# Attention values in two float16 parts with a power-of-two scale per head pair, reciprocals taken for two steps at once, and a new table of constants

## The chip, the cores and the metric

The kernel runs on one core of a Trainium2 chip. The core has five engines that run beside each other, each through its own list of instructions in order: TensorE (PE in the profile; its weight loads, PEld, overlap its matmuls), VectorE (DVE), ScalarE (ACT), GpSimd (POOL) and SyncE (SP), which issues nearly all DMAs here. The metric is the device time of one execution in microseconds (us), the lower the better. With one core there is one span, from the first to the last instruction that the profiler saw.

## The reference, cut to what matters

```python
# q, k, v: (4, 8, 576, 64) float32; tau 0.02; weights drawn as float64: w_in (512, 2048), w_out (2048, 512), two sets
def _attn_ref(q, k, v, tau):
    scores = q @ k.T / np.sqrt(64)
    thresh = scores.max(-1) - tau
    scores = np.where(scores >= thresh, scores, -1e9)
    attn = np.exp(scores - scores.max(-1))
    attn = attn / (attn.sum(-1) + 1e-09)
    return attn @ v
x = attn_out.transpose(0, 2, 1, 3).reshape(2304, 512)
x = np.maximum(x @ w_in, 0) ** 2 @ w_out                 # first layer
h = x @ w_in2;  return np.maximum(0.01 * h, h) @ w_out2  # second layer
```

A score is kept if it lies within tau of its row's largest; the softmax is over what is kept.

## The kernel before, in words

**Attention.** The 32 heads are taken as 16 head pairs (4 batches of 4 pairs), and a pair as 9 steps of 128 query rows (four per head, and one in which the last 64 rows of both heads lie together), 144 steps in all. `step` is one of them: TensorE makes 128x576 scores (`s`), VectorE takes the row maximum negated (`nb`, L539), ScalarE the exponential (`e`, L540), VectorE or GpSimd the threshold (`th`, L541 or L542), VectorE in one instruction masks and sums (`e` and `sum`, L544), then `t` = (sum + 1e-9)/32768 (`UP` is 32768; L547), and VectorE its reciprocal `r` (L549). The scaled row is split in two float16 parts `P` (high, then low as e\*r minus high, L587, or by two instructions at L297 to L310), and SyncE issues a DMA that transposes both parts into `PT`.

**Values.** Pairs 0 to 5 are in `nat`: scores in full float32 from `KH` alone. Pairs 6 to 15 have their q and k split in two parts each (`Q`, `KH` and `KL`). Pairs 0 to 4 (`nav` is 5) multiply the probabilities with `v` in float32, transposed on TensorE (L565, L566, L631). The other 11 pairs have `v` in three bfloat16 parts: the upper halves of `VA` and of `VA`'s remainder lie side by side as 128 columns, and the third part is `VB`, 64 columns. `prep` makes them with two subtractions over 128x640 that GpSimd or VectorE does. `values` is called for each head and each of its two column ranges (256 and 320 query rows), 44 times for these 11 pairs. Its list of products:

```python
        prods = [(slice(0, P), slice(0, w), j, hi, j) for j in range(NH)]
        prods += [(slice(0, P), slice(0, w), NH + j, hi, j) for j in range(MAIN)]
        prods += [((lo3, up3)[j % 2], slice(0, w), j, low, j) for j in range(MAIN)]
        prods += [(r, c_, MAIN, low, MAIN) for r, c_ in ((lo3, slice(0, half)), (up3, slice(half, w)))]
```

The first two lines are nine matmuls of 128 weight columns; the last two are six of 64, which go by turns to the two halves of the PSUM bank `o` (a ring of one). ScalarE then copies one half out (`tmp`, L639), VectorE adds the other (`xs`, L644), and SyncE writes `x1d` in DRAM.

**Layers.** All products of the layers are three passes of two-part operands. d_ff is 16 blocks. While attention runs, `ffn` does blocks 0 to 11 (`NFA`) of the first layer for the first 1792 tokens, in 7 pieces of 256 tokens (L675 is h, L701 is y), as fillers of TensorE. Behind the attention, the second phase (L811 h, L857 y) does all 16 blocks for the last 512 tokens, the missing blocks 12 to 15 for the others, and the second layer. Weights come as float64 and are put together from their two 32-bit words (`w_block`: L349, L350, L352, L354, then a rounded copy and the rest).

**Order.** No order is written by hand. `Plan.order` takes every operation with its assumed cost on each engine that may do it, and a priority, and lays them out one after the other; an engine with several choices is weighed by `price`. The program's order on each engine is the result, and it is fixed at build time. So a change in `CFG` or in a cost moves instructions everywhere.

Of the kernel before, what the change touches and what calls it, by code (L numbers as in the profile page):

```python
# [63 lines left out]
class Plan:  # L64
# [32 lines left out]
    def order(self):  # L97
# [58 lines left out]
        while len(done) < len(self.ops):  # L156
# [47 lines left out]
            else:  # L204
# [5 lines left out]
                free[e] = o.end - OVER.get(e, 0.0)  # L210
# [29 lines left out]
def mm(n):  # L240
    return (n + 5.5) / 2400.0
# [15 lines left out]
def tile_kernel(ctx: ExitStack, tc: tile.TileContext, qT, kT, vv, w1, w2, tau, eye, out):  # L257
# [25 lines left out]
    const.tile([P, 40], F32, name="rim")  # L283
# [40 lines left out]
    ca = const.tile([P, 1], F32, name="ca")  # L324

# [613 lines left out]
```

## Time and profile before

| what | value |
|---|---|
| runs before, us | 1086.04, 1094.08, 1093.3 (median 1093.3) |
| the profiled execution's own time, us | 1087.9 |
| its span, us | 1086.1 |
| granted TensorE clock over the span | 1.000 |
| PE busy, us (share) | 1059.4 (98%) |
| DVE busy, us | 732.8 (67%) |
| ACT busy, us | 509.1 (47%) |
| POOL busy, us | 342.1 (31%) |

The times are of whole executions; the span of the profiled one is 1.8 us less than its own time. The shares are means over parts of the program that have different limits: attention with fillers, and then layers alone. Matmuls are pipelined, so the durations of neighbours overlap; how far apart two of them start tells what one takes.

### The profile page before, as it was taken

What the parts mean: (1) busy time and instruction counts of PE and PEld (TensorE: products, weight loads), DVE (VectorE), ACT (ScalarE), POOL (GpSimd) and SP (SyncE); (2) the same over time, 40 slices, a digit from 0 to 9 for tenths busy, and PEclk for the clock granted to TensorE, in tenths of its full rate; (3) what the DMA queues carried; (4) which work ended last, traced back from release to release, by engine and by line L of the source; (5) the groups of instructions that cost most, each with busy time, mean ns of one, the idle gap of its engine ahead of it and who ended that gap; (6) DMA issues with size and microseconds to landing.
All of it is one profiled execution on the core that took longest, in us unless ns stands there. A gap on an engine that the chain in (4) does not pass through costs nothing.

```text
span 1086.1 us, 17711 instructions
## 1 busy us (share of the span) xinstructions
PE 1059.4 (98%) x6343; PEld 886.1 (82%) x6343; DVE 732.8 (67%) x1557; ACT 509.1 (47%) x902; POOL 342.1 (31%) x421
## 2 busy tenths in 40 slices
PE   8988999999999999999999999999999999999998
PEld 4555778888998889989888888888888888888887
DVE  7999898788988898756999975763423433433343
ACT  6899878876776788735343431221211111111121
POOL 5765778889886676410000000000000000000000
PEclk9999999999999999999999999999999999999999
DMA  7444449998888896745644543610100100010010
GB/s 196 122 133 144 137 108 193 181 171 171 169 171 149 172 169 119 142 83 180 227 138 155 181 147 123 225 41 0 70 8 1 39 20 1 1 40 1 1 40 20
DMA packets 186983, 119.16 MB, mean 110 GB/s; under 512 B 146064, under 2 KB 164624, under 8 KB 186896
## 3 DMA queue, kind: packets, MB, share of 16 engines
q1 hardware_dynamic: 186528, 117.82, 44.3%
q8 instruction: 50, 0.82, 0.3%
q10 hardware_dynamic: 368, 0.21, 0.1%
q14 instruction: 37, 0.30, 0.1%
HBM read 70.98 MB, written 17.83 MB: 82 GB/s over the span
## 4 chain that ended last, share of the span: by engine, by line
PE 65%; DVE 1%; ACT 1%; issue 0%; POOL 0%; ACTq 0%; POOLq 0%; DVEq 0%
PE h L811 26%; PE y L857 26%; PE h L675 5%; PE y L701 5%; PE o L627 2%; PE s L529 2%; DVE e L544 0%; DVE nb L539 0%; DVE P L308 0%; ACT e L540 0%; ACT P L554 0%; DVE gl L308 0%; DVE P L587 0%; ACT tmp L639 0%; POOL t L547 0%
## 5 line engine op out<-in xcount | busy, mean ns | idle before, releaser
L823 DVE TENSOR_TENSOR r<-h,r 128x512 f32<-128x512 f32 (+1 forms) x80 | 51.0, 638 | 211.4 <-ACT r L822 211.4
L822 ACT ACTIVATE r<-h 128x512 f32<-128x512 f32 (+1 forms) x80 | 44.5, 557 | 313.1 <-PE h L811 310.6
L310 POOL TENSOR_TENSOR xl<-xr,xh 128x512 fp32r<-128x512 f32 (+1 forms) x11 | 12.7, 1157 | 418.3 <-ACT xh L297 253.5
L544 DVE SCALAR_TENSOR_TENSOR e<-s,th,e 128x576 f32<-128x576 f32 x144 | 116.8, 814 | 31.5 <-ACT e L540 27.4
L529 PE MATMUL s<-KH,Q 128*128 128x288 f32 (+1 forms) x440 | 121.1, 368 | 10.1 <-DVE e L544 6.6
L540 ACT ACTIVATE e<-s,nb 128x576 f32<-128x576 f32 x144 | 106.7, 742 | 38.5 <-DVE nb L539 22.5
L539 DVE TENSOR_REDUCE nb<-s 128x1 f32<-128x576 f32 x144 | 107.8, 750 | 12.4 <-PE s L529 11.3
L529 PEld LDWEIGHTS s<-KH,Q 128*128 128x128 f32 (+1 forms) x440 | 73.6, 183 | 30.6 <-issue 12.3
L308 DVE TENSOR_TENSOR gl<-r,gh 128x512 fp32r<-128x512 f32 (+1 forms) x129 | 85.6, 664 | 8.2
L587 DVE SCALAR_TENSOR_TENSOR P<-e,r,P 128x576 f16<-128x576 f32 x59 | 57.1, 970 | 2.8 <-ACT P L554 1.7
L819 ACT ACTIVATE r<-h 128x512 f32<-128x512 f32 (+1 forms) x32 | 18.2, 573 | 86.4 <-PE h L811 80.1
L627 PE MATMUL o<-PT,VA 128*128 128x320 f16 (+1 forms) x396 | 56.5, 287 | 0.4 <-DVE xs L644 0.4
L529 PE MATMUL s<-KL,Q 128*128 128x288 f32 x200 | 55.8, 294 | 0.0
L299 DVE CAST gh<-r 128x512 fp32r<-128x512 f32 (+1 forms) x103 | 43.8, 425 | 15.9 <-ACT r L684 7.8
L310 POOL TENSOR_TENSOR gl<-r,gh 128x512 fp32r<-128x512 f32 (+1 forms) x25 | 32.7, 1309 | 58.7 <-issue 45.2
L352 DVE SCALAR_TENSOR_TENSOR wraw<-wraw 128x512 int32<-128x512 int32 x64 | 48.9, 765 | 1.7 <-ACT wraw L349 0.6
L349 ACT ACTIVATE wraw<-wraw 128x512 f32<-128x512 f32 x64 | 43.0, 681 | 9.9 <-DMA wraw<-w 9.7
L354 DVE SCALAR_TENSOR_TENSOR wraw<-wraw 128x512 int32<-128x512 int32 x64 | 45.9, 717 | 0.6
L542 POOL TENSOR_SCALAR th<-nb,ca 128x1 f32<-128x1 f32 x75 | 33.3, 444 | 37.0 <-DVE nb L539 29.3
L627 PEld LDWEIGHTS <-VA 128*128 128x128 bf16 x396 | 35.2, 98 | 10.8 <-issue 0.4
L554 ACT ACTIVATE e<-e,r 128x576 f32<-128x576 f32 x51 | 39.4, 776 | 7.5 <-DVE r L549 6.9
L310 POOL TENSOR_TENSOR P<-e,P 128x576 f16<-128x576 f32 x29 | 38.7, 1339 | 8.5 <-ACT P L297 7.6
(616 smaller groups left out, 3044.5 us busy)
## 6 DMA issues: line engine op xcount, KB each, us to landing
wraw<-w SPq DMA_DIRECT2D x64, 512.0 KB, 4.1
wraw<-qT SPq DMA_DIRECT2D x20, 288.0 KB, 4.2
wraw<-kT SPq DMA_DIRECT2D x20, 288.0 KB, 4.4
out<-yo SPq DMA_DIRECT2D x18, 256.0 KB, 2.0
VA<-vv SPq DMA_DIRECT2D x32, 128.0 KB, 2.8
x2d<-yo SPq DMA_DIRECT2D x16, 256.0 KB, 3.3
xr<-x2d SPq DMA_DIRECT2D x4, 1024.0 KB, 5.8
y1d<-ys SPq DMA_DIRECT2D x14, 256.0 KB, 2.8
```

What stands on the lines that cost most here:

```text
L308: alts.append(("V", dve(n), lambda: nc.vector.tensor_tensor(out=o(), in0=a(), in1=b(), op=alu), kind + "*"))
L310: alts.append(("G", pool2(n), lambda: nc.gpsimd.tensor_tensor(out=o(), in0=a(), in1=b(), op=alu), kind))
L529: nc.tensor.matmul(ps.get()[r, g, 0:S2], lhsT=o.Q.get()[:, q], rhs=(kk.get() if o.KL else f32(kk.get()))[:, g_(g)], start=k == 0 or not o. ...
L539: op(("V", 0.75, lambda: nc.vector.tensor_reduce(out=nb.get(), in_=pv(), axis=AX.XY, op=ALU.max, negate=True)), [ps], [nb], i + CFG["pd1"] ...
L540: op(("A", 0.74, lambda: nc.scalar.activation(e.get(), pv(), AF.Exp, bias=nb.get(), scale=1.0)), [ps, nb], [e], i + CFG["pex"], True)
L544: op(("V", 0.82, lambda: nc.vector.scalar_tensor_tensor(out=e.get(), in0=pv(), scalar=th.get(), in1=e.get(), op0=ALU.is_ge, op1=ALU.mult, ...
L587: op(("V", 0.8, lambda: nc.vector.scalar_tensor_tensor(out=lo(), in0=ev(), scalar=r_.get(), in1=hi(), op0=ALU.mult, op1=ALU.subtract), "*" ...
L627: nc.tensor.matmul(ps.get()[r, c_], lhsT=f_(v), rhs=parts16(pt)[:, j, c_], start=(k == 0), stop=k >= len(prods) - 2)
L675: nc.tensor.matmul(ps.get()[:, i], lhsT=a.get()[:, kc * P:(kc + 1) * P], rhs=x.get()[:, kc], start=(i == 0 and q == 0 and kc == 0), stop=( ...
L701: nc.tensor.matmul(yp[m // 2].get()[:, m % 2], lhsT=a.get()[:, c], rhs=x.get()[:, i], start=(f + i == 0 and q == 0 and m % 2 == 0), stop=( ...
L811: nc.tensor.matmul(ps.get()[:, 0:n], lhsT=a.get()[:, kc * P:(kc + 1) * P], rhs=x.get()[:, kc, 0:n], start=(q == 0 and kc == 0), stop=(q == ...
L857: nc.tensor.matmul(o(), lhsT=l, rhs=r, start=(first and q == 0), stop=(last and q == 2))
```

## The change

- **Values.** `prep` now only loads `VA`; a new `split`, called four steps into the pair before, makes two float16 parts of v. VectorE takes the largest absolute value of each partition (`vmax`), TensorE adds these over the partitions (a matmul with a 128x128 tile of ones into the bank `o`), VectorE makes a power of two of it (`vbound`) and its reciprocal (`vscale`), and the inverse scale (`vback`) is applied where `values` copies out. The products are nine matmuls a call; the six of `VB` are gone.
- **Reciprocals.** `sum`, `t` and `r` are 128x2 and serve two steps. `step` makes the even step's sum, the odd step's `t` and `r` are for both, and what follows (`rest`) is recorded behind the odd step. `th` is one subtraction.
- **Scale of the scores.** It is no longer multiplied into k by an instruction of its own for the split pairs (`wraw` by `qsc`, L416 or L417), but into q where q is rounded, and the rest of q is one VectorE instruction (it was GpSimd's or VectorE's).
- **Choice of engine.** The first conversion step of weights may go to GpSimd, their rounding too.
- **Constants.** All of `CFG`; `eb` (buffers of `e`) is 4, and was 3; `nf` gives 8 blocks for the last 256-token piece in the first phase, the other 4 go to the second phase; `xsg0` and `xsg` let ScalarE and GpSimd do more of the copies out (`xs`).

```diff
-    pd1=0.001, pex=-0.455, pd2=0.23, ph=4.551, pl=-0.358, hu=False, bg=2.696, lead=3.299, w0=24.867, wstep=2.436, fend=1.021, tol=0.448,
-    hor=-0.24, xlead=5.45, nb=3, eb=3, pb=3, ptb=3, kvb=3, nat=[0, 1, 2, 3, 4, 5], nav=5, two=False, vb=2, tmb=1, gb=2, xb=1, w2step=0.586,
+    lead1=1.422, xsg0=[1, 2], lbm=8, lb=[[1, 3, 7], [0], [1, 4], [0, 1, 6]], xsm=4, xsg=[1, 2], dq=1.924, xu=False, pqk=-4.818, pd1=-0.132,
+    pex=0.418, pd2=-0.108, ph=4.738, pl=-0.721, hu=False, bg=5.042, lead=4.267, w0=19.675, wstep=2.136, fend=1.005, tol=0.271, hor=-0.444,
+    xlead=5.567, nb=3, eb=4, pb=3, ptb=3, kvb=3, nat=[0, 1, 2, 3, 4, 5], nav=5, two=False, vb=2, tmb=1, gb=2, xb=1, w2step=-1.195,
+    nf=[12, 12, 12, 8], wo=1.672, slack=0, slackd=0.939, wrb=3, r1b=1, xrb=1,
...
-            op(times(kr.get, 2 * S), [kr], [kr], at(2))
             for h in range(2):
-                op(rnd(lambda h=h: qs(h), lambda h=h: q3()[:, h], S), [qr], [Q], at(2))
+                op(times(lambda h=h: qs(h), S, lambda h=h: q3()[:, h]), [qr], [Q], at(2))
             for h in range(2):
-                op(sub(lambda h=h: qs(h)[D:P], lambda h=h: q3()[D:P, h], lambda h=h: f32(qs(h)[D:P]), S), [qr, Q], [Q], at(3 + h))
+                op(("V", dve(S), lambda h=h: nc.vector.scalar_tensor_tensor(
+                    out=qs(h)[D:P], in0=q3()[D:P, h], scalar=qsc[D:P], in1=f32(qs(h)[D:P]), op0=ALU.mult, op1=ALU.subtract), "*"), [qr, Q], [Q], at(3 + h))
...
-        op(sub(lambda: va.get()[:, :, :, 1], lambda: va.get()[:, :, :, 0], lambda: up()[:, :, :, 0], nv), [va], [va], at(11))
-        op(sub(lambda: vb.get(), lambda: va.get()[:, :, :, 1], lambda: up()[:, :, :, 1], nv), [va], [vb], at(13))
+        op(("V", dve(nv), lambda: nc.vector.tensor_reduce(out=mx.get(), in_=va.get(), axis=AX.XYZ, op=ALU.max, apply_absolute_value=True)), [va], [mx], at(10))
+        st = val("ps_o", "o", 1, [P, 512], F32)
+        op(("T", 0.25, lambda: nc.tensor.matmul(st.get()[:, 0:1], lhsT=ones, rhs=mx.get(), start=True, stop=True)), [mx, ones_v], [st], at(10))
+        op(("V", 0.15, lambda: nc.vector.tensor_scalar(out=bd.get(), in0=st.get()[:, 0:1], scalar1=1e-25, scalar2=2.0 ** -14, op0=ALU.max, op1=ALU.mult)), [st], [bd], at(10))
+        op(("V", 0.15, lambda: nc.vector.tensor_scalar(out=bd.get().bitcast(I32), in0=bd.get().bitcast(I32), scalar1=0x7F800000, scalar2=None, op0=ALU.bitwise_and)), [bd], [bd], at(10))
+        op(("V", 0.158, lambda: nc.vector.reciprocal(out=sc.get(), in_=bd.get())), [bd], [sc], at(10))
...
+           [va, sc], [v16], at(11))
+        op(("V", dve(nv), lambda: nc.vector.scalar_tensor_tensor(out=v2(), in0=va.get(), scalar=sc.get(), in1=v1(), op0=ALU.mult, op1=ALU.subtract), "*"),
+           [va, sc, v16], [v16], at(13))
...
-        op([(g, c_, lambda eng=eng: eng.tensor_scalar(out=t_.get(), in0=sm.get(), scalar1=1e-9, scalar2=1.0 / UP, op0=ALU.add, op1=ALU.mult), "t")
-            for g, c_, eng in (("V", 0.146, nc.vector), ("G", 0.19, nc.gpsimd))], [sm], [t_], i + CFG["pd2"], True)
-        op(("V", 0.158, lambda: nc.vector.reciprocal(out=r_.get(), in_=t_.get())), [t_], [r_], i + CFG["pd2"], True)
+        if k:
+            op([(g, c_, lambda eng=eng: eng.tensor_scalar(out=t_.get(), in0=sm.get(), scalar1=1e-9, scalar2=1.0 / UP, op0=ALU.add, op1=ALU.mult), "t")
+                for g, c_, eng in (("V", 0.148, nc.vector), ("G", 0.192, nc.gpsimd))], [sm], [t_], i + CFG["pd2"], True)
+            op(("V", 0.16, lambda: nc.vector.reciprocal(out=r_.get(), in_=t_.get())), [t_], [r_], i + CFG["pd2"], True)
+        return lambda: rest(i, n, h, t, o, ps, e, r_, k)
...
         def av(k0, k1):
             for k in range(k0, k1):
-                r, c_, j, f_, v = prods[k]
-                nc.tensor.matmul(ps.get()[r, c_], lhsT=f_(v), rhs=parts16(pt)[:, j, c_], start=(k == 0), stop=k >= len(prods) - 2)
+                nc.tensor.matmul(ps.get()[:, 0:w], lhsT=o.V16.get()[:, k if k < NH else k - NH, h].rearrange("p a d -> p (a d)"),
+                                 rhs=parts16(pt)[:, k, 0:w], start=(k == 0), stop=(k == NB - 1))
```

What it moves is seen in the order of the built programs. On TensorE, a call of `values` with 320 columns among layer matmuls, before (`s` scores, `o` the output bank, `w0ih` a weight block's part; the nine pairs of rows on `VA` stand once, and of the six on `VB` the first and the last):

```order
L675 MATMUL h<-xh,w0ih 128x256 x4
L627 LDWEIGHTS VA
L627 MATMUL o<-PT,VA 128x320
...
L627 LDWEIGHTS VB
L627 MATMUL o<-PT,VB 64x320
...
L627 MATMUL o<-PT,VB 64x160
L529 MATMUL s<-KH,Q_1831 128x288
```

and now, where the one-column matmul for a later pair's scale stands a little ahead of such a call:

```order
L733 MATMUL y_2561<-gh,w9ol 128x256
L507 MATMUL o<-vmax,ones 128x1
L556 MATMUL s<-KH,Q_2498 128x288
L556 MATMUL s<-KL,Q_2498 128x288
...
L654 LDWEIGHTS V_2774
L654 MATMUL o<-PT,V_2774 128x320
...
L733 MATMUL y_2553<-gh,w10oh 128x256
```

The rows on `VB` have gone, and a row on `vmax` and `ones` has come, in the same bank.

On VectorE, some steps in the middle of attention, before (numbers are buffers):

```order
L539 TENSOR_REDUCE nb_3606<-s_3592 128x1
L308 TENSOR_TENSOR P16_2_110<-e_3546,P16_2_110 128x576
L549 RECIPROCAL r_3632<-t_3617 128x1
L539 TENSOR_REDUCE nb_3636<-s_3614 128x1
L544 SCALAR_TENSOR_TENSOR e_3622,sum_3655<-s_3592,th_3624,e_3622 128x576
L547 TENSOR_SCALAR t_3670<-sum_3655 128x1
L549 RECIPROCAL r_3676<-t_3670 128x1
L544 SCALAR_TENSOR_TENSOR e_3658,sum_3678<-s_3614,th_3666,e_3658 128x576
```

and now:

```order
L505 TENSOR_REDUCE vmax_3505<-VA_3355 128x1
L620 SCALAR_TENSOR_TENSOR P16_1_110<-e_3357,r_3409,P16_1_110 128x576
L579 RECIPROCAL r_3528<-t_3514 128x2
L573 SCALAR_TENSOR_TENSOR e_3495,sum_3533<-s_3449,th_3497,e_3495 128x576
L566 TENSOR_REDUCE nb_3544<-s_3507 128x1
L508 TENSOR_SCALAR vbound_3554<-o_3542 128x1
L568 TENSOR_TENSOR th_3562<-ca_81,nb_3544 128x1
L509 TENSOR_SCALAR vbound_3554<-vbound_3554 128x1
L566 TENSOR_REDUCE nb_3565<-s_3548 128x1
L510 RECIPROCAL vscale_3575<-vbound_3554 128x1
L573 SCALAR_TENSOR_TENSOR e_3560,sum_3533<-s_3507,th_3562,e_3560 128x576
L577 TENSOR_SCALAR t_3593<-sum_3533 128x2
```

One reciprocal of two columns stands for two steps (both `e` rows add to `sum_3533`), and the chain for the scale of `v` is threaded through the steps of the pair before.

## Rows read from the trace of the kernel before

**Rows 1.** Busy time by stage: us, PE, PEld, DVE, ACT, POOL, PEclk, DMA share, GB/s

```profile
0.00:142.00 142.00, 126.81 (x725) 80.86 (x726) 123.28 (x288) 120.22 (x200) 92.98 (x137) 1.00 0.50 144
142.00:471.00 329.00, 322.03 (x2589) 288.15 (x2589) 280.37 (x665) 247.25 (x452) 243.46 (x276) 1.00 0.83 159
471.00:526.00 55.00, 54.25 (x447) 51.81 (x446) 35.84 (x69) 23.20 (x41) 2.44 (x4) 1.00 0.52 158
526.00:1086.00 560.00, 556.33 (x2587) 465.32 (x2585) 293.28 (x539) 118.41 (x211) 3.19 (x4) 1.00 0.20 67
```

**Rows 2.** Who waited for whom, 142 to 471 us: total, times, longest

```profile
DVE e L544 <- ACT e L540: 24.2, 41, 2.0
```

**Rows 3.** Timeline of TensorE around one 320-column call: start, us, instruction

```profile
267.13 1.40 PE L627 MATMUL o<-PT,VA 128*128 128x320 f16 x9
268.46 0.53 PE L627 MATMUL o<-PT,VB 128*64 128x320 f16 x6
268.92 0.39 PE L701 MATMUL y<-gh,w1oh 128*128 128x256 f32 x1
269.14 0.28 PE L701 MATMUL y<-gl,w1oh 128*128 128x256 f32 x1
269.26 0.28 PE L701 MATMUL y<-gh,w1ol 128*128 128x256 f32 x1
```

**Rows 4.** The same, behind a 256-column call

```profile
291.12 0.47 PE L627 MATMUL o<-PT,VB 128*64 128x256 f16 x6
291.51 0.39 PE L675 MATMUL h<-xh,w9ih 128*128 128x256 f32 x1
```

**Rows 5.** Groups by line and shape, whole span: busy us, mean ns, idle before

```profile
L627 PE MATMUL o<-PT,VB 128*64 128x320 f16 x88 | 10.2, 311 | 0.0
L627 PE MATMUL o<-PT,VB 128*64 128x256 f16 x88 | 9.0, 285 | 0.0
```

**Rows 6.** Timeline of TensorE in the first stage: float32 transposes

```profile
62.53 0.60 PE L565 MATMUL pt<-eye_sb,e 128*128 128x128 f32 x4
62.97 0.27 PE L566 MATMUL pt<-eye_sb,e 128*128 128x128 f32 x1
```

**Rows 7.** Groups of VectorE by line and shape, 142 to 471 us

```profile
L587 DVE SCALAR_TENSOR_TENSOR P<-e,r,P 128x576 f16<-128x576 f32 x58 | 56.3, 973 | 2.8 <-ACT P L554 1.7 <-POOL P L553 0.9
L549 DVE RECIPROCAL r<-t 128x1 f32<-128x1 f32 x99 | 15.7, 159 | 2.9 <-POOL t L547 1.1
L541 DVE TENSOR_SCALAR th<-nb,ca 128x1 f32<-128x1 f32 x59 | 12.4, 211 | 0.6
L644 DVE SCALAR_TENSOR_TENSOR xs<-o,tmp 64x320 f32<-64x320 f32 x21 | 10.0, 478 | 3.8 <-ACT tmp L639 3.1
L547 DVE TENSOR_SCALAR t<-sum 128x1 f32<-128x1 f32 x64 | 9.4, 148 | 1.0
L644 DVE SCALAR_TENSOR_TENSOR xs<-o,tmp 64x256 f32<-64x256 f32 x21 | 8.7, 412 | 3.0 <-ACT tmp L639 2.8
L308 DVE TENSOR_TENSOR Q<-wraw,Q 64x576 fp32r<-64x576 f32 x3 | 3.5, 1150 | 0.1
```

**Rows 8.** Busy time by stage, one stretch of the second stage

```profile
250.00:300.00 50.00, 49.37 (x405) 45.15 (x404) 47.22 (x115) 34.85 (x63) 43.69 (x49) 1.00 0.88 170
```

**Rows 9.** Timeline of VectorE: the low part of P twice

```profile
260.74 0.80 DVE L587 SCALAR_TENSOR_TENSOR P<-e,r,P 128x576 f16<-128x576 f32 x1
262.56 1.47 DVE L587 SCALAR_TENSOR_TENSOR P<-e,r,P 128x576 f16<-128x576 f32 x1
```

**Rows 10.** Timeline of GpSimd at the second of these

```profile
262.13 1.28 POOL L310 TENSOR_TENSOR gl<-r,gh 128x512 fp32r<-128x512 f32 x1
```

**Rows 11.** Groups of GpSimd by line and shape, 142 to 471 us

```profile
L310 POOL TENSOR_TENSOR Q<-wraw,Q 64x576 fp32r<-64x576 f32 x17 | 27.0, 1594 | 2.0 <-DVE Q L299 0.8
```

**Rows 12.** Timeline of VectorE: the last part of the second phase's first input

```profile
513.04 0.68 DVE L308 TENSOR_TENSOR xl<-xr,xh 128x512 fp32r<-128x512 f32 x1
```

**Rows 13.** Timeline of TensorE: the second phase's first matmuls

```profile
518.79 1.09 PE L811 MATMUL h<-xh,w0ih 128*128 128x512 f32 x4
```

More of the change, by code (lines that the diff above doesn't have):

```diff
@@ L209, in order @@
                     o.end = port["V"] = max(o.end, port["G"] - 0.13 + cost[o])
-                free[e] = o.end - OVER.get(e, 0.0)
+                free[e] = o.end - (OVER.get(e, 0.0) if o.alts[0][3:] != ("x",) else 0.0)
             for g, *_ in o.alts:
@@ L324, in tile_kernel @@
     ca = const.tile([P, 1], F32, name="ca")
+    ones = const.tile([P, P], F32, name="ones")
+    ones_v = Val()
     eye_v = Val()
@@ L492, in prep @@
             return
-        op(sub(lambda: va.get()[:, :, :, 1], lambda: va.get()[:, :, :, 0], lambda: up()[:, :, :, 0], nv), [va], [va], at(11))
-        op(sub(lambda: vb.get(), lambda: va.get()[:, :, :, 1], lambda: up()[:, :, :, 1], nv), [va], [vb], at(13))
+        v16 = o.V16 = val("att", "V16", CFG["vb"], [P, NH, 2, 2, D], F16)
+        mx, bd, sc, us = (val("small", r, 2, [P, 1], F32) for r in ("vmax", "vbound", "vscale", "vback"))
+        o.us = us
+        op(("V", dve(nv), lambda: nc.vector.tensor_reduce(out=mx.get(), in_=va.get(), axis=AX.XYZ, op=ALU.max, apply_absolute_value=True)), [va], [mx], at(10))
@@ L544, in step @@
+        k = i % 2
+        if not k:
+            sums[:] = [val("small", r, 3, [P, 2], F32) for r in ("sum", "t", "r")]
+        sm, t_, r_ = sums
         op(("V", 0.82, lambda: nc.vector.scalar_tensor_tensor(
-            out=e.get(), in0=pv(), scalar=th.get(), in1=e.get(), op0=ALU.is_ge, op1=ALU.mult, accum_out=sm.get())),
+            out=e.get(), in0=pv(), scalar=th.get(), in1=e.get(), op0=ALU.is_ge, op1=ALU.mult, accum_out=sm.get()[:, k:k + 1])),
            [ps, th, e], [e, sm], i + CFG["pd2"], True)
-        op([(g, c_, lambda eng=eng: eng.tensor_scalar(out=t_.get(), in0=sm.get(), scalar1=1e-9, scalar2=1.0 / UP, op0=ALU.add, op1=ALU.mult), "t")
-            for g, c_, eng in (("V", 0.146, nc.vector), ("G", 0.19, nc.gpsimd))], [sm], [t_], i + CFG["pd2"], True)
@@ L739, in tile_kernel @@
             oT = op(("N", 0.0, open1), [], [], i, after=[o for o in plan.ops if any(v.ring == "pt" for v in o.vals)])
+        weights(i)
         if i in begin and steps[i][0] + 1 < len(order):
             prep(steps[i][0] + 1)
-        step(i)
-        while jb < NA and avail[jb] <= i:
-            now[0] = max(now[0], avail[jb])
-            ffn(jb, clock)
-            jb += 1
+        rests.append(step(i))
+        if i % 2:
+            for r in rests:
+                r()
+            rests = []
+            for n in range(len(order)):
+                if n in pairs and not hasattr(pairs[n], "cut") and i >= (begin[n - 1] + 4 if n else 0):
+                    pairs[n].cut = True
+                    split(n)
+    weights(10 * NS)
     att_ops = list(plan.ops)
-    while jb < NA:
-        now[0] = max(now[0], NS)
+    for jb in range(NA):
+        now[0] = max(now[0], min(avail[jb], NS))
         ffn(jb, clock)
-        jb += 1
     attn = [o for o in att_ops if any(v.ring in ATT for v in o.vals)]
```

113 lines of the change are left out of this document (60 added, 53 removed).

## The prediction

> **What bounds the kernel now.** I read the busy time by stage first [rows 1]. Behind 526 us TensorE works for 556.33 of 560 us and VectorE for 293.28: this stage is TensorE's alone. From 471 to 526 us it is the same (54.25 of 55). From 142 to 471 us TensorE is busy for 322.03 of 329 us, with VectorE at 280.37, ScalarE at 247.25 and GpSimd at 243.46: TensorE sets the pace there, since the layers' matmuls fill what attention leaves, and the long wait of VectorE is for exponentials (24.2 us in 41 waits) [rows 2]. Up to 142 us no layer work is there for most of the time; TensorE shows 126.81 of 142 us, VectorE 123.28, ScalarE 120.22. There the chain of the softmax, mainly on VectorE, sets the pace. So a matmul taken out behind 142 us should come off the end nearly whole, as long as nothing else is nearly full; in that stage VectorE is the next one.
>
> **The products with VB.** They are what the change removes from TensorE. In a 320-column call the six of them start at 268.46 and the next product at 268.92, so they take 0.46 us; in a 256-column call 291.12 to 291.51, 0.39 us [rows 3, 4]. (The nine in front take 1.33 us, so these six, four full and two half passes, would be 0.74 us if none ran beside another.) The 88 rows of either width, four a call, make 22 calls of each [rows 5]: 22 x (0.46 + 0.39) = 18.7 us. The first layer matmul behind a call takes 0.22 us where the next takes 0.12 [rows 3]; that stays, since nine 16-bit products stand ahead of it as before. Of the 44 calls 41 lie between the 46th and the 144th row maximum, which is the stage from 142 to 471 us: 41 x 0.425 = 17.4 us there, 1.3 us behind it. No other engine hides this: TensorE has no gap in these rows.
>
> **The matmuls on vmax.** Eleven come, of one column, in float32. No row shows one. The nearest are the float32 transposes of 128 columns, four of which start within 0.44 us (62.53 to 62.97) [rows 6], 0.11 us each: the low end is 11 x 0.11 = 1.2 us. It stands among layer matmuls, so it may bring the 0.10 us of a change of kind twice. It also holds the only bank `o`: it waits until the output before has been copied out, and the next call of `values` waits until VectorE has read `vbound`. TensorE takes its list in order, so behind either wait everything is late, scores too. A copy out behind a call is about 0.45 us (0.478 and 0.412) [rows 7], so the high end is 0.31 + 0.45 + 0.2 of waits, some 1 us: 11 us. I take 0.3 us, 3.3 in all, nearest to the transposes with the two changes of kind, because the order puts layer matmuls or scores between this matmul and the next call. Scores, transposes and layer products are as many as before; four blocks of 256 tokens go from the first phase to the second at the same 0.12 us a matmul, 96 x 0.12 = 11.5 us each way, net zero.
>
> **VectorE from 142 to 471 us.** By the order, counted between the same row maxima, with means from [rows 7]. Reciprocals 99 to 49: -50 x 0.159 = -8.0. `t` 64 to 21: -43 x 0.148 = -6.4. `th` 59 to 56, now without a second scalar, so like `t`: -12.4 + 8.3 = -4.1. `xs` 42 to 17: -18.7 + 7.6 = -11.1. The rest of q 3 to 20, and it can't go to GpSimd any more: 20 x 0.95 less 3.5 = +15.5 (between 0.75, from a low part of P of 576 columns at 0.80, and the 1.15 of [rows 7]: 11.5 to 19.5). The low part of P 58 to 71: 13 x 0.97 = +12.6 (10.4 at the short 0.80). For v: 10 maxima of 640 columns and 11 low parts, about 0.85 each by the same row, and 35 instructions of one column at 0.15, +23. Conversions, scalings and subtractions that went elsewhere: some -10. Sum +11.5, so 292 us, between 284 and 301. The stage would be 329 - 17.4 + 3.0 (ten of the eleven small matmuls) = 314.6 us, so VectorE would be busy for 93% of it. In the stretch from 250 to 300 us it is busy for 47.22 of 50 us, 94%, and TensorE still for 49.37 [rows 8]: it can be so full and keep up. I take 2 us of loss; up to 9 at the high end (301 at 93% is 324 us).
>
> What the trace shows of collisions is this. The low part of P takes 0.80 us at 260.74, and 1.47 at 262.56, where GpSimd runs a 1.28 us subtraction from 262.13 to 263.41 [rows 9, 10]; the mean of 58 is 0.973 [rows 7]. [...] The rows weigh it: 0.973 against 0.80 is 0.17 of 0.67, so a quarter of them meet one now. GpSimd also loses its 27.0 us of subtractions for q in this stage [rows 11] and its 19 of 128x640, so I keep the present mean and no longer one.
>
> **The first stage.** VectorE loses 22 reciprocals (-3.5), 4 `xs`, some `t` and `th` (-2.5), and gets four weight remainders, one more conversion and the first pair's maximum (+7): nearly zero. ScalarE gives some 10 us of conversions to GpSimd. The even step of a pair waits for the sum of the odd one, a step of some 2.8 us (142 us over some 45 steps is at most 3.2); a fourth buffer of `e` covers that, and without it VectorE's next mask would wait. I take 0, with 4 us either way.
>
> **The turn to the second phase.** The last input of the second phase is ready at 513.04 + 0.68 = 513.72, and its first matmul starts at 518.79 [rows 12, 13], 5.1 us later. Between the last call of `values` and that matmul 240 layer matmuls stood, now 204: 36 x 0.12 = 4.3 us less cover. 0.8 us are left, so 0, at worst some 2 us. Behind it TensorE is the bound with VectorE at half; conversions that went to GpSimd have all of a 560 us stage.
>
> **Sum.** Of the profiled execution's 1087.9 us: -18.7 + 3.3 + 2 + 0 + 0 = 1074.5, -13.4 us. The median of the three runs lies 5.4 us above the profiled one, whose time is near the low end. A new median may fall at either place, 1074.5 or 1079.9; I say 1077 us.
>
> **Rivals.** (1) VectorE becomes the bound between 142 and 471 us. For it: 93% by the sum above, and in the first stage, where it does set the pace, it only reaches 123.28 of 142 us, 87%. Against it: [rows 8]. With 301 us of work at 93% the stage shrinks by 5 us and not by 14; with the 1.3 us behind it the gain is some 6 us: 1082 to 1087. (2) Slower: the chain for the scale of v stops TensorE. The maximum stands in VectorE's list between the steps' instructions, and TensorE's matmul on it in a fixed place; if VectorE runs late, this matmul waits, the scores behind it wait, and VectorE then lacks scores. It eats all of the 18.7 us at 1.7 us a pair; at 2.7 us, one row maximum and two masks behind, it is 11 x 2.7 = 30 us against 18.7: 1099 to 1104. Against it: the order spreads the chain, with over ten of the steps' instructions between the maximum and the low part of v on VectorE, so a late link has others ahead of its use. (3) The first stage shrinks too: ScalarE's 10 us less and shorter chains let VectorE be as full there as in [rows 8], 123.28/0.94 = 131 us, 11 us less: 1064 to 1069. (4) TensorE is not full, and what is taken out is swallowed: 1087.9 + 3.3 = 1091. For it: the busy time counts overlapping durations, and weight loads fill only 288.15 of 329 us. Against it: layer matmuls of 256 columns start 0.12 us apart in [rows 3] with none missing between, and the one behind VB starts only after it. [...]
>
> **How the numbers follow.** Forecast 1070 to 1082: 0.50. Rival 1, 1082 to 1088: 0.26. Rival 2, above 1095: 0.08. Rival 3, below 1070: 0.13. Rival 4, 1091: 0.03. The likeliest is the forecast, 1077. For eight in ten I leave out rival 2 and what lies below rival 3's own bound: 1064 to 1091. About 1% (11 us) is what the measurement can tell from no change: the three runs lie within 8 us. Faster by over 1% is below 1082.4: the forecast and rival 3, 0.63; within 1% are rivals 1 and 4, 0.29; slower is rival 2, 0.08.
>
> **What would show it.** Right: no L627-like rows of 64 columns, calls of `values` at 1.33 us and then layer matmuls; TensorE's last first-phase work some 25 us earlier (14 from the stage, 11.5 moved on), the second phase 11.5 us longer; VectorE at 91 to 94% between the 46th and 144th row maximum. Wrong: TensorE idle for over 10 us there with waits for `e`, `vmax` or `xs` (rivals 1 and 2), a matmul on `vmax` that takes over 1 us up to the next one, or a first stage that moves by over 4 us.

## The result, and the profile after

The changed kernel takes 1096.35 us (median of 19 runs, 1093.16 to 1098.87), the kernel before 1088.24 (19 runs beside it). The ratio is 1.0062, 95% interval [1.0049, 1.0074]: some 7 us slower (8 by the medians), where 1077 us was forecast, 11 us faster. The profiled execution has a span of 1094.3 us; before it was 1086.1.

Busy time by stage of the kernel after, cut at the same places of the program as [rows 1] (46th and 144th row maximum; columns as there):

```profile
0.00:149.00 149.00, 132.29 (x734) 85.01 (x735) 134.45 (x276) 110.71 (x186) 98.95 (x139) 0.98 0.49 142
149.00:473.00 324.00, 298.45 (x2303) 274.82 (x2303) 311.18 (x616) 237.73 (x435) 203.73 (x268) 1.00 0.80 156
473.00:527.00 54.00, 52.47 (x409) 49.76 (x407) 34.53 (x53) 23.63 (x42) 18.80 (x17) 1.00 0.56 160
527.00:1094.00 567.00, 563.27 (x2661) 472.82 (x2659) 306.36 (x467) 120.72 (x218) 111.02 (x93) 1.00 0.20 68
```

In the second stage VectorE is busy for 311.18 of 324 us, 96%, and TensorE for 298.45, where it was 322.03 of 329. The stage is 5 us shorter, the one in front 7 us longer. The cuts and the start of the second phase stand in the timelines of VectorE and TensorE:

```profile
149.22 0.75 DVE L566 TENSOR_REDUCE nb<-s 128x1 f32<-128x576 f32 x1
473.15 0.75 DVE L566 TENSOR_REDUCE nb<-s 128x1 f32<-128x576 f32 x1
520.60 1.09 PE L848 MATMUL h<-xh,w0ih 128*128 128x512 f32 x4
```

Groups of VectorE in the second stage, for [rows 7] (busy us, mean ns of one):

```profile
L620 DVE SCALAR_TENSOR_TENSOR P<-e,r,P 128x576 f16<-128x576 f32 x71 | 66.2, 940 | 1.2 <-ACT P L587 0.8 <-POOL P L586 0.2
L568 DVE TENSOR_TENSOR th<-ca,nb 128x1 f32<-128x1 f32 x56 | 21.7, 394 | 0.7
L479 DVE SCALAR_TENSOR_TENSOR Q<-wraw,qsc,Q 64x576 fp32r<-64x576 f32 x20 | 20.1, 1008 | 0.6
L518 DVE SCALAR_TENSOR_TENSOR V<-VA,vscale,V 128x640 f16<-128x640 f32 x11 | 15.2, 1381 | 0.0
L577 DVE TENSOR_SCALAR t<-sum 128x2 f32<-128x2 f32 x21 | 11.3, 537 | 0.5
L505 DVE TENSOR_REDUCE vmax<-VA 128x1 f32<-128x640 f32 x10 | 8.1, 805 | 0.1
L579 DVE RECIPROCAL r<-t 128x2 f32<-128x2 f32 x49 | 7.7, 156 | 0.4
```

The thresholds and `t`, of one and two columns, are the ones to look at. A threshold of one column takes 394 ns on the mean (211 before), `t` of two columns 537 (148 for one before), while the reciprocal of two columns takes 156. The timelines of VectorE and, below, of GpSimd show when:

```profile
158.84 0.16 DVE L568 TENSOR_TENSOR th<-ca,nb 128x1 f32<-128x1 f32 x1
174.98 1.72 DVE L568 TENSOR_TENSOR th<-ca,nb 128x1 f32<-128x1 f32 x1
199.64 1.23 DVE L568 TENSOR_TENSOR th<-ca,nb 128x1 f32<-128x1 f32 x1
202.92 0.15 DVE L568 TENSOR_TENSOR th<-ca,nb 128x1 f32<-128x1 f32 x1
```

```profile
159.78 0.19 POOL L568 TENSOR_TENSOR th<-ca,nb 128x1 f32<-128x1 f32 x1 [4.39 <-DVE nb L566]
175.28 1.41 POOL L310 TENSOR_TENSOR KL<-wraw,KH 128x576 fp32r<-128x576 f32 x1
199.28 1.57 POOL L310 TENSOR_TENSOR gl<-r,gh 128x512 fp32r<-128x512 f32 x1
```

At 158.84 GpSimd stands idle (4.39 us before 159.78) and the threshold takes 0.16 us. The thresholds that start at 174.98 and 199.64 end at 176.70 and 200.87, just as GpSimd's subtractions do (176.69 and 200.85): they wait for GpSimd's instruction to end. Counted over the whole trace, 35 of VectorE's 71 thresholds take over 250 ns, and each of them ends less than 50 ns behind the end of a GpSimd instruction; the 19 with nothing on GpSimd beside them take 160 ns at most. The same holds for `t` of two columns: 14 of 30 take over 250 ns and end at most 0.12 us behind a GpSimd instruction, here at 301.75 behind 301.73:

```profile
300.56 1.19 DVE L577 TENSOR_SCALAR t<-sum 128x2 f32<-128x2 f32 x1
300.30 1.42 POOL L310 TENSOR_TENSOR KL<-wraw,KH 128x576 fp32r<-128x576 f32 x1 [1.41 <-ACT KH L297]
```

The waits of TensorE for score banks in the second stage (total us, times, longest), in the kernel before and now:

```profile
PE s L529 <- DVE e L544: 5.6, 9, 1.2
PE s L556 <- DVE e L573: 20.2, 29, 3.0
```

The scores now wait for VectorE's mask, which frees the bank `s`, over three times as long as before. The timeline of TensorE at a matmul on `vmax` and at a call of `values`, for [rows 3]:

```profile
180.01 0.28 PE L507 MATMUL o<-vmax,ones 128*128 128x1 f32 x2
180.15 0.36 PE L733 MATMUL y<-gh,w8oh 128*128 128x256 f32 x1
249.13 1.38 PE L654 MATMUL o<-PT,V 128*128 128x320 f16 x9 [0.26 <-DVE vbound L508]
250.25 0.39 PE L733 MATMUL y<-gh,w10oh 128*128 128x256 f32 x1
250.47 0.28 PE L733 MATMUL y<-gl,w10oh 128*128 128x256 f32 x1
250.59 0.28 PE L733 MATMUL y<-gh,w10ol 128*128 128x256 f32 x1
```

The products with VB are gone, and a call takes 1.12 us. From its first product to the third layer matmul behind it are 1.46 us, and in [rows 3] 2.13: the call is shorter by 0.67 us, not by the 0.46 of the prediction. The matmul on `vmax` takes 0.14 us in six of eleven cases; in the other five, scores come next and start 0.26 to 1.07 us behind it. On TensorE the change takes away more than the prediction counted.

### The profile page after: what moved, and what is told of

It reads as the page before. It is cut to its first block, busy times and chain, and to the rows that moved or that the text cites. A ratio compares the mean times of both kernels' runs of the same rounds, so it can differ in the third digit from the quotient of the medians.

```text
span 1094.3 us, 17166 instructions
## 1 busy us (share of the span) xinstructions
PE 1046.5 (96%) x6101; PEld 882.4 (81%) x6101; DVE 786.5 (72%) x1409; ACT 492.8 (45%) x879; POOL 432.5 (40%) x515
## 4 chain that ended last, share of the span: by engine, by line
PE 63%; DVE 18%; issue 4%; ACT 4%; DMA 2%; POOL 1%; SPq 0%; DVEq 0%; ACTq 0%; POOLq 0%
PE y L894 26%; PE h L848 26%; DVE e L573 4%; DVE nb L566 4%; PE y L733 3%; PE h L707 3%; DVE P L620 3%; PE s L556 3%; ACT e L567 1%; PE o L654 1%; DVE th L568 1%; DVE t L577 1%; DMA PT<-P 1%; DVE Q L479 1%; DVE wraw L357 1%
## 5 line engine op out<-in xcount | busy, mean ns | idle before, releaser
L310 POOL TENSOR_TENSOR gl<-r,gh 128x512 fp32r<-128x512 f32 (+1 forms) x53 | 79.0, 1491 | 181.3 <-DVE gh L299 153.2
L310 POOL TENSOR_TENSOR xl<-xr,xh 128x512 fp32r<-128x512 f32 (+1 forms) x24 | 34.4, 1433 | 119.8 <-ACT xh L297 118.3
L308 DVE TENSOR_TENSOR gl<-r,gh 128x512 fp32r<-128x512 f32 (+1 forms) x103 | 70.1, 680 | 13.0 <-ACT gh L297 5.4
L355 DVE SCALAR_TENSOR_TENSOR wraw<-wraw 128x512 int32<-128x512 int32 x64 | 59.3, 928 | 3.0 <-POOL wraw L352 1.1
L654 PE MATMUL o<-PT,V 128*128 128x320 f16 (+1 forms) x396 | 57.6, 287 | 3.5 <-DVE xs L674 1.7
L357 DVE SCALAR_TENSOR_TENSOR wraw<-wraw 128x512 int32<-128x512 int32 x64 | 55.2, 864 | 0.9
L297 ACT CAST gh<-r 128x512 fp32r<-128x512 f32 (+1 forms) x66 | 39.9, 607 | 27.8 <-DVE r L857 18.3
L654 PEld LDWEIGHTS <-V 128*128 128x128 f16 x396 | 35.0, 98 | 14.5 <-issue 3.7
L353 DVE TENSOR_SCALAR wraw<-wraw 128x512 int32<-128x512 int32 x64 | 44.6, 699 | 1.0 <-DMA wraw<-w 1.0
L568 POOL TENSOR_TENSOR th<-ca,nb 128x1 f32<-128x1 f32 x73 | 26.5, 363 | 45.0 <-DVE nb L566 37.6
L352 POOL TENSOR_SCALAR wraw<-wraw 128x512 f32<-128x512 f32 x33 | 29.4, 893 | 27.0 <-DMA wraw<-w 27.0
```

The costliest lines, as they stand in the source:

```text
L308: alts.append(("V", dve(n), lambda: nc.vector.tensor_tensor(out=o(), in0=a(), in1=b(), op=alu), kind + "*"))
L310: alts.append(("G", pool2(n), lambda: nc.gpsimd.tensor_tensor(out=o(), in0=a(), in1=b(), op=alu), kind))
L355: op(("V", 0.69, lambda ui=ui, yi=yi: nc.vector.scalar_tensor_tensor(out=yi(), in0=ui(), scalar=3, in1=yi(), op0=ALU.logical_shift_left, o ...
L357: op(("V", 0.69, lambda ui=ui, yi=yi: nc.vector.scalar_tensor_tensor(out=yi(), in0=ui(), scalar=-(1 << 31), in1=yi(), op0=ALU.bitwise_and, ...
L654: nc.tensor.matmul(ps.get()[:, 0:w], lhsT=o.V16.get()[:, k if k < NH else k - NH, h].rearrange("p a d -> p (a d)"), rhs=parts16(pt)[:, k, ...
```

## The experiments

The order of each engine stays as it was, except in the runs of which it is said that the planner made another. Ratios are to runs of the kernel before beside each on the same chip, with medians of 1089.0 to 1091.4 us. The diffs are shortened.

**The form of the threshold and of `t`.** VectorE's threshold alone goes back to one tensor input, with `ca` as its second scalar:

```diff
-("V", 0.15, nc.vector.tensor_tensor(out=th, in0=ca, in1=nb, op=subtract))
+("V", 0.15, nc.vector.tensor_scalar(out=th, in0=nb, scalar1=-1.0, scalar2=ca, op0=mult, op1=add))
```

> The changed kernel with one instruction form undone: VectorE's threshold is again a one-column TENSOR_SCALAR and not a TENSOR_TENSOR of two SBUF inputs; the order of all engines stays. Lock theory (VectorE sets the pace from 0 to 473 us, and its new tiny instructions wait for whole GpSimd instructions): the 71 rows of th on VectorE, 394 ns in the mean in the second stage and 575 in the first, go back to some 210 ns without a tail, VectorE loses 14 to 18 us of work, and the time falls by 9 to 16 us against the changed kernel. Volume theory (the large new instructions for q and v on VectorE are the cost, the tiny ones only fill its waits): the rows get shorter, but the time moves by under 3 us. Pairing theory (the even step waits for the odd one's sum): no change.

1088.78 us, ratio 0.9994 [0.9979, 1.0009]: 7.6 us less than the changed kernel, short of the 9 to 16 of the lock theory and clear of the 3 of the others. The second edit splits VectorE's `t` in its place:

```diff
-("V", 0.148, nc.vector.tensor_scalar(out=t, in0=sm, ...))
+("V", 0.148, for q in 0, 1: nc.vector.tensor_scalar(out=t[:, q:q+1], in0=sm[:, q:q+1], ...))
```

> The changed kernel, with VectorE's t of two columns made by two TENSOR_SCALARs of one column each; all else as in the changed kernel. Lock theory: the 30 rows of 128x2 (537 ns and 417 ns in the mean, up to some 1.5 us) become 60 rows of some 150 ns with no tail, some 10 us less on VectorE with 4 us of new instructions, so 4 to 9 us less than the changed kernel. Volume and pairing theories: within 3 us of the changed kernel, or slower by the 30 instructions more (up to 3 us).

1090.59 us, ratio 1.001 [0.9996, 1.0023]: 5.8 us less than the changed kernel, as the lock theory said. Both edits together:

> Both edits in one kernel. Lock theory: the gains add, 13 to 24 us less than the changed kernel, so 1072 to 1083 us, below the kernel before; VectorE's busy time from the 46th to the 144th row maximum falls from 311 to some 293 us, and the first stage (46th row maximum at 149.2 us) comes back to some 143 us. Volume theory: within 4 us of the changed kernel. Pairing theory: the first stage stays at 149 us.

1080.64 us, ratio 0.9918 [0.9894, 0.9943]: some 9 us faster than the kernel before, and 15.7 us faster than the changed one, as the lock theory said; the volume theory allowed 4 us, and the pairing theory kept the first stage at 149 us, where it is 143.3. This version beats both kernels. Its second stage, its start of the second phase and three groups of VectorE:

```profile
143.00:458.00 315.00, 297.34 (x2303) 275.75 (x2302) 297.09 (x637) 236.92 (x434) 207.50 (x268) 0.99 0.85 161
```

```profile
505.80 1.09 PE L852 MATMUL h<-xh,w0ih 128*128 128x512 f32 x4
```

```profile
L568 DVE TENSOR_SCALAR th<-nb,ca 128x1 f32<-128x1 f32 x56 | 11.3, 210 | 0.7
L518 DVE SCALAR_TENSOR_TENSOR V<-VA,vscale,V 128x640 f16<-128x640 f32 x11 | 10.4, 945 | 0.1
L580 DVE TENSOR_SCALAR t<-sum 128x1 f32<-128x1 f32 x42 | 5.2, 146 | 0.0
```

The reverse, the kernel before with only its threshold in the new form:

```diff
-("V", 0.21, nc.vector.tensor_scalar(out=th, in0=nb, scalar1=-1.0, scalar2=ca, op0=mult, op1=add))
+("V", 0.21, nc.vector.tensor_tensor(out=th, in0=ca, in1=nb, op=subtract))
```

> The kernel before with the new form put in: VectorE's 69 thresholds are a TENSOR_TENSOR of two SBUF inputs, all else and the order as before. Lock theory: those rows go from 211 ns to 350 to 500 ns with single ones over 1 us, VectorE gets 9 to 15 us more work; as TensorE sets the pace behind 142 us and VectorE is busy for 85% there, part of it is hidden: 2 to 8 us slower than the kernel before. Volume and pairing theories: rows of some 160 ns, the time within 1 us of the kernel before or a little less.

1101.34 us, ratio 1.011 [1.0089, 1.013]. The group of VectorE over the whole span:

```profile
L541 DVE TENSOR_TENSOR th<-ca,nb 128x1 f32<-128x1 f32 x69 | 45.7, 664 | 0.8
```

One line of one-column instructions, 664 ns on the mean where it was 211, costs 12 us there, where 2 to 8 were expected, and more than in the changed kernel; GpSimd was busier before (243.46 of 329 us against 203.73 of 324), which fits, but wasn't varied by itself. Whether it is two columns or two adjacent ones was asked with the first edit and a spaced `t`:

```diff
-tensor_scalar(out=t, in0=sm, ...)                     # tiles of two columns
+tensor_scalar(out=t[:, 0:3:2], in0=sm[:, 0:3:2], ...) # tiles of four, every second one used
```

> The changed kernel with VectorE's threshold as a one-scalar-pointer instruction again (as in the run on the threshold alone, 1088.8 us), and the pair's sums, t and reciprocals kept in every second column of a tile of four, so that VectorE's `t` still has two columns but not adjacent ones. If it is the form of two adjacent columns that waits for GpSimd, `t` falls from 537 ns to some 110 to 160 ns and the time to that of both edits together, 1080.6 us (1079 to 1083). If any two-column instruction waits, or if the pairing of the steps costs the time, `t` stays near 540 ns and the time at 1088.8 us (1087 to 1091).

1088.17 us, ratio 0.9978 [0.9962, 0.9995], as with the first edit alone, and `t` in the second stage:

```profile
L578 DVE TENSOR_SCALAR t<-sum 128x2 f32<-128x2 f32 x21 | 10.2, 485 | 0.5
```

So two columns of `t` wait, adjacent (537 ns) or not (485); one column doesn't (146 ns), and neither does the reciprocal of two (156 ns).

**What TensorE's work is worth.** The kernel before without its products with VB, the order kept:

```diff
-for k in range(k0, k1):
+for k in range(k0, min(k1, NH + MAIN)):
```

> The kernel before without its six products with VB in each call (the third part of v is left out of the product; its subtraction and everything else stay, the order of the other engines word for word). This is the first term of the prediction by itself: 44 x 0.425 = 18.7 us off TensorE. If TensorE set the pace there, 15 to 19 us go: 1070 to 1074 against 1089. If VectorE and its waits nearly set it already, the gain is a part, as in the run with the products put back: 5 to 9 us, 1080 to 1084.

1083.48 us, ratio 0.9924 [0.9896, 0.9953]: 6 us by the medians, 8 by the ratio, not 18.7. The 46th and the 144th row maximum, before and then in this run:

```profile
142.53 0.76 DVE L539 TENSOR_REDUCE nb<-s 128x1 f32<-128x576 f32 x1
470.95 0.75 DVE L539 TENSOR_REDUCE nb<-s 128x1 f32<-128x576 f32 x1
142.44 0.75 DVE L539 TENSOR_REDUCE nb<-s 128x1 f32<-128x576 f32 x1
468.78 0.75 DVE L539 TENSOR_REDUCE nb<-s 128x1 f32<-128x576 f32 x1
```

The second stage, from which 17.4 us were to go, is 2.1 us shorter in these two executions (326.3 us for 328.4). Busy time between the times of [rows 1], and the waits there:

```profile
142.00:471.00 329.00, 305.68 (x2365) 282.96 (x2364) 278.67 (x667) 246.61 (x455) 245.22 (x278) 0.99 0.83 159
```

```profile
DVE e L544 <- ACT e L540: 28.4, 42, 4.3
PE s L529 <- DVE e L544: 16.6, 22, 3.6
```

TensorE is busy for 16.4 us less in the same 329 us and waits for the mask, 16.6 us where it was 5.6, while VectorE's wait for exponentials, 24.2 us in [rows 2], has grown. The reverse, in the version with both edits: the six products put back in front of each call.

```diff
+for k in range(6):
+    nc.tensor.matmul(ps[half(k % 2), cols(k)], lhsT=V16[:, k % NH, h, 0], rhs=parts16(pt)[:, k % NH, cols(k)], start=True, stop=True)
 for k in range(k0, k1):
```

> Both edits (1080.6 us), and in front of each of the 44 calls the six products of 64 columns that the change removed are issued again on 16-bit operands into the same bank, which the first real product then restarts: the work that was taken from TensorE is put back, 44 x 0.425 = 18.7 us, and nothing else changes. If TensorE sets the pace as the prediction said, 18 to 19 us come back: 1098 to 1100. If VectorE does, TensorE has the room (299 of 317 us busy between 143 and 460 us) and only a part comes back, 2 to 8 us: 1083 to 1089.

1088.74 us, ratio 0.9983 [0.9967, 0.9999], 7 to 8 us above the version with both edits. The time taken off is more than 18.7 us: among layer matmuls, from the one before a call to the third behind it, a 320-column call takes 2.25 us before and 1.59 without the products with VB, a 256-column one 1.94 and 1.35. By these, 22 x (0.66 + 0.59) = some 27 us go, as an estimate from the calls that stand so; the products put back take 0.55 and 0.49, some 23 us. So a quarter to a third of TensorE's time shows. To see what keeps the rest, the kernel before with a shorter row maximum (over 288 of 576 columns):

```diff
-nc.vector.tensor_reduce(out=nb, in_=pv(), axis=XY, ...)
+nc.vector.tensor_reduce(out=nb, in_=pv()[:, 0:1], axis=XY, ...)
```

> The kernel before, with the row maximum taken over half of the 576 columns (the other half's scores are left out of it), the order word for word the same: VectorE has some 0.35 us less in each step, 99 x 0.35 = 35 us between the 46th and the 144th row maximum. If TensorE alone set the pace there, this stage keeps its 328 us within 2 us. If the chain through VectorE set it too, the stage shrinks by what TensorE leaves, 310 of 317 us busy, some 4 to 7 us. The stage in front shrinks in both cases, by up to 45 x 0.35 = 16 us.

1087.54 us, ratio 0.9964 [0.9937, 0.999]. The maximum falls to 451 ns, 43 us less over the span, and some 4 us are gained. The second stage keeps its time (327.6 us for 328.4), and so does the first, against both alternatives (144.1 us for 142.5). With the VB products left out as well:

> The same shorter row maximum, and no products with VB (the third part of v is left out of the product as well). If the chain through VectorE kept back what the VB products gave, it can't here: the stage between the 46th and the 144th row maximum is shorter than in the run with the short maximum alone by 14 to 18 us, where it was 2 us without it. If TensorE's own waits keep it back, the difference stays at 2 to 5 us.

1078.71 us, ratio 0.9882 [0.9844, 0.992], 9 us below the run before it, and the second stage 321.7 us for 327.6. VB is worth 9 us with the short maximum and 6 to 8 with the long one, so in the kernel before the length of the row maximum isn't what kept the rest; VectorE's other work wasn't shortened. The last run on this lets the planner lay out a new order for the calls without VB:

```diff
-op(("T", passes * mm(w) + 0.22 * (k == NH + MAIN), ...
+op(("T", passes * mm(w) if k < NH + MAIN else 0.01, ...
```

> The kernel before without its products with VB (the third part of v is left out of the product), and the planner told so: the order is laid out anew for the shorter calls. If the old order kept back the rest of the 18.7 us, 15 us and more go now: 1071 to 1076. If the order as such decides, the time lies anywhere within 15 us of the run with the old order, 1083.5 us.

1078.28 us, ratio 0.9888 [0.9863, 0.9913]: 12 us. That the old order kept back the 4 to 6 us more isn't shown by this: an order alone moves the time by as much (below).

**What VectorE's work is worth** in the version with both edits. First the maximum of v over 8 of 640 columns:

```diff
-tensor_reduce(out=mx, in_=va, axis=XYZ, op=max, apply_absolute_value=True)
+tensor_reduce(out=mx, in_=va[:, 0, :, 0:4], axis=XY, op=max, apply_absolute_value=True)
```

> Both edits (1080.6 us), with the maximum of v taken over 8 of its 640 columns: the order of all engines stays word for word, the chain with its matmul stays, only VectorE's maximum gets shorter, from 0.81 us to 0.15 at the least, 11 x 0.65 = 7 us of VectorE's time. If VectorE sets the pace, 4 to 7 us go: 1074 to 1077. If the order and its waits do, as the run without the maximum could mean, nothing goes: 1079 to 1082.

1076.62 us, ratio 0.9862 [0.9834, 0.989]. The group is 7.3 us shorter (8.9 before the edit), the time 4 us by the medians and 6 by the ratios:

```profile
L505 DVE TENSOR_REDUCE vmax<-VA 128x1 f32<-128x8 f32 x11 | 1.6, 149 | 0.1
```

Then the shared reciprocal undone in its place:

```diff
-nc.vector.reciprocal(out=r, in_=t)
+for q in 0, 1: nc.vector.reciprocal(out=r[:, q:q+1], in_=t[:, q:q+1])
```

> Both edits (1080.6 us), with the shared reciprocal of a pair undone in its place: two reciprocals of one column where one of two columns stood, the order otherwise word for word. VectorE gets 72 more instructions, 8 to 11 us by 0.11 to 0.157 us each. If VectorE sets the pace, all of it is seen: 1088 to 1092. If TensorE does, 0 to 3 us: 1080 to 1084.

1083.1 us, ratio 0.9934 [0.9909, 0.996]: about 2 us, and the intervals overlap. Two of one column follow each other so closely that the 72 instructions more cost 4.8 us of busy time, not 8 to 11 (with both edits, and here):

```profile
L583 DVE RECIPROCAL r<-t 128x2 f32<-128x2 f32 x72 | 11.3, 156 | 0.7
L585 DVE RECIPROCAL r<-t 128x1 f32<-128x1 f32 x144 | 16.1, 149 | 0.3
```

**What the order alone does.** The kernel before with one assumed length of the planner (0.22 above, of the products with VB) at 0.18 and at 0.26, and no instruction changed:

> The kernel before, with no instruction added, removed or changed; only the planner's assumed length of the products with VB is 0.04 us shorter, so that it lays out another order. If the time follows the sums of work, it stays within 3 us of the kernel before, 1087 to 1093. If the order decides, it moves by 5 us and more.

1088.72 us, ratio 0.9983 [0.9968, 0.9998].

> The same with the assumed length 0.04 us longer. If the time follows the sums of work, 1087 to 1093; if the order decides, it moves by 5 us and more, and not by as much or in the same direction as with the shorter length.

1096.13 us, ratio 1.005 [1.0026, 1.0074]. So the same work in another order lies 2 us below or 5 us above. The version with both edits and the planner told 0.21 for VectorE's threshold and 0.25 for `t`:

> Both edits (1080.6 us), and the planner told what VectorE's two instructions cost: threshold 0.21 instead of 0.15 us, the pair of `t` 0.25 instead of 0.148. The work is the same, only the order and the choice of engines move (some thresholds and `t` to GpSimd). If the sum of VectorE's work sets the time, it stays within 3 us: 1078 to 1084. If the order itself does, as the run without the maximum could mean, it moves by 10 us and more either way.

1092.8 us, ratio 1.0017 [0.9996, 1.0038], 11 us above the same kernel in the order of the change. With the scale of v fixed, which leaves out the maximum, its matmul and the bound:

```diff
-tensor_reduce(out=mx, ...); matmul(st[:, 0:1], lhsT=ones, rhs=mx); bd = max(st, 1e-25) * 2**-14; bd &= 0x7F800000
+nc.gpsimd.memset(bd, 2.0 ** -12)
```

> Both edits (1080.6 us), with the scale of v fixed at 2^12 by GpSimd: no vmax, no matmul on it, no bound; the scale found on the chip is left out. VectorE loses 10 maxima of 0.81 us and some 20 instructions of 0.1 to 0.15 us in the stage, about 10.5 us. If VectorE sets the pace there, 8 to 11 us go: 1070 to 1073. If TensorE does, the eleven matmuls at 0.3 us go: 1077 to 1078. If the chain stops TensorE at each pair, 1.7 us or more a pair go, 19 us and more: below 1062.

1100.27 us, ratio 1.0095 [1.0065, 1.0126]: 20 us slower with less work. All three alternatives miss. The planner made another order; with the order kept, the short maximum (above) gives its 4 to 6 us. The new order isn't shown to be all of it. The second stage is 13 us longer than with both edits, with a granted clock of 0.96 in it (0.99 there). The second phase is 9 us longer with the same matmuls at a granted clock of 1.00: those of 512 columns start 231 ns apart, with both edits 227. Why isn't known. The method of the change under the constants of the kernel before:

```diff
-price=..., lb=[[1, 3, 7], [0], [1, 4], [0, 1, 6]], eb=4, xsg=[1, 2], bg=5.042, nf=[12, 12, 12, 8], ...
+price=..., lb=[[0, 1, 3, 4, 7], [0, 1, 3, 7], [3, 5], [2, 3, 5, 7]], eb=3, xsg=[], bg=2.696, nf=[12, 12, 12, 12], ...
```

> Both edits (1080.6 us), with the planner's constants of the kernel before and all four blocks of layer work at twelve groups in the first phase, as there: the method of the change without its new constants. VectorE gets 25 of its `xs` back (+11 us) and some subtractions of layer work, and gives up 15 low parts of P (-14 us). If VectorE sets the pace, the time follows its sum of work, within 5 us of 1080.6 or above it up to 1090. If TensorE does, its 18.7 us less show here as well: 1073 to 1079.

1120.69 us, ratio 1.0276 [1.0249, 1.0304]. Busy time from 100 to 150 us, with both edits and here:

```profile
100.00:150.00 50.00, 47.09 (x322) 36.95 (x321) 47.01 (x92) 38.02 (x65) 33.35 (x38) 1.00 0.54 147
100.00:150.00 50.00, 44.15 (x272) 31.16 (x271) 29.89 (x71) 31.55 (x52) 25.82 (x39) 0.97 0.29 76
```

No engine is full there, where VectorE had 47.01 us in the order of the change; that the engines wait for each other in turn is argued from this. The granted clock over the span is 0.986, with both edits 0.997. Which of the constants does it wasn't tried.

## Why the prediction was wrong

**The step that turned the sign: `th` "now without a second scalar, so like `t`: -4.1", and `t` -6.4.** I priced both by rows of other forms. A threshold with two tensor inputs was to cost 148 ns and cost 394; a `t` of two columns was to cost what one column costs and cost 537. In the second stage that is 21.7 + 11.3 us where 8.3 + 3.1 stood in the sum. Shown: with both put back the time falls by 15.7 us, the first stage from 149.2 to 143.3 us included. Some 2 of these go with the clock: the executions with a granted clock of 1.000 take 1093.2 to 1093.5 us as changed (four) and 1079.8 and 1080.0 with both edits. In [rows 9, 10] an instruction of VectorE was slowed beside one of GpSimd, and the prediction weighed that by the low part of P alone, not for the 56 thresholds and 21 `t` of this stage. One column is enough for it: with two tensor inputs the same 69 thresholds of the kernel before take 664 ns on the mean, with one 211. `t` has one tensor input and takes long with two columns, adjacent (537 ns) or spaced (485), and not with one (146 ns). Why two columns of `t` wait and a reciprocal of two (156 ns) doesn't, no run shows.

**The largest term: -18.7 us for the products with VB, "nearly whole".** Its size was too small: counted from the first of them to the next product, the six took 0.46 and 0.39 us, but a call is shorter by 0.66 and 0.59: the nine in front, 1.33 us up to the first of the six in [rows 3], take 1.12 in a 320-column call as changed. Even so the time moved by 6 to 8 us with the order kept, 12 with a new one, 7 to 8 in the reverse. The reading that failed is "TensorE sets the pace there": 322.03 of 329 us busy showed a list that the layers' matmuls filled, not an engine for which nothing else was late. With VB gone the scores wait for banks (16.6 us). I took VectorE's wait for exponentials as slack; it is part of the loop of score, maximum, exponential, mask and bank, and grew. That the length of VectorE's row maximum keeps the rest was tried and falls. What remains is the loop through four lists whose order is fixed; which link ends last wasn't settled. Rival 4 had this effect and a chance of 0.03; its sign, weight loads in only 288.15 of 329 us, was set aside for the spacing of the layer matmuls, which stand as close (0.12 us at 250.47) where something else is late.

**VectorE, 292 us between 284 and 301.** 311.2 as changed, 297.1 with both edits: apart from `th` and `t` and the low part of v (1.381 us for an estimated 0.85, 0.945 with both edits) the sum held; the low parts of P at 0.940 and the rest of q at 1.008 met their estimates. With both edits rival 1 comes nearer: VectorE is busy for 297.09 of 315 us, and 7.3 us less on it give 4 to 6. But TensorE's products put back show too, so neither engine sets the pace alone.

**The blocks moved, "net zero".** The second phase is 1094.3 - 520.6 = 573.7 us, and was 1086.1 - 518.8 = 567.3: 6.4 us paid (11.5 was said). By the count of matmuls, 48 of the 96 came newly to lie behind that cut (240 of 256 columns on `h` before, 288 now; on `y` 96 both times), 5.8 us at 0.12. The other side, less TensorE work in the first phase, couldn't come back where TensorE didn't set the pace.

**What held.** The first stage, 0 within 4 us, only with both edits: 143.3 us for 142.5. The changed kernel has 149.2, and of the 5.9 us between, 3.8 lie ahead of the tenth row maximum (29.0 us, with both edits 25.2), where only the changed kernel's execution shows a lower clock (0.66 from 10 to 20 us); how much of it is the two forms isn't shown. And the reason given, that the chain "mainly on VectorE" sets the pace there, fails: with the short row maximum the stage doesn't shrink. The turn to the second phase, 0: from the 144th maximum 47.5 us, as 47.8 before. The matmul on `vmax` at 0.3 us was 0.14 among layer matmuls. Slower had a chance of 0.08 by rival 2, and came by another way: TensorE waits for `vbound` 0.3 us in the second stage, and the short maximum gives no more than its own time. The 2.5 us added for the median rested on three runs; 19 give 1088.24 us for the kernel before, close to its profiled execution. Summed with both edits: +0.8 - 13.4 - 0.4 + 6.4 = -6.6 us of span, which is 1079.5 for 1086.1. The -13.4 of the second stage can't be divided between the method and its order, since the method in the order of the old constants is 39 us slower.

## What to carry to other kernels

Price an instruction by the row of its own form, not of its size: here a threshold of one column on VectorE took 210 ns with one tensor input and 394 to 664 with two, a TENSOR_SCALAR 146 ns with one column and 474 to 537 with two, and in the changed kernel those over 250 ns ended with an instruction of GpSimd. An engine that is busy for 98% among fillers isn't shown to set the pace (of some 27 us taken off TensorE 6 to 8 came off the time); take work off it, order kept, before counting on it. Where a planner makes the order, an edit of 0.04 us in its table moved the time by 2 us down and 5 us up here, so a gain below that needs the same order on both sides.

## What was not expected of the hardware

Instructions of one or two columns on VectorE take from 150 ns up to 1.86 us (`th`) and 2.15 us (`t`), by their form and by what GpSimd runs beside them (means 394 and 664 ns with two tensor inputs, 210 with one tensor and a scalar column; 474 to 537 with one tensor of two columns, 146 with one column; reciprocals 149 to 158 either way). And the granted clock of TensorE, in two stretches of the changed kernel:

```profile
5.00:10.00 5.00, 2.56 (x11) 1.63 (x10) 3.00 (x6) 1.94 (x4) 0.38 (x2) 1.00 1.10 315
10.00:20.00 10.00, 9.64 (x34) 6.02 (x33) 7.26 (x19) 6.06 (x9) 4.46 (x7) 0.66 0.74 199
```

It was 1.00 up to 10 us and has a mean of 0.66 in the next 10, with 0.50 from 12 to 18 us. In the 5 us ahead of it TensorE worked for 2.56 us; the kernel before worked for 3.36 there and kept 1.00. What lowered it, no run shows. This lies in the first 20 us, where the tenth row maximum came 1.7 us later than before (29.0 and 27.3 us).
